# Cosformer attention and channel/token mixer on one core: the first three batches and two MLPs written as one explicit list of operations

## The chip, the cores and the metric

The kernel runs on 1 core of one Trainium2 chip. The metric is device time in microseconds (us) of one execution, the median of several. Before: 278.84 us, median of 3 runs (278.72 to 279.54). Executions of one kernel scatter by 0.7% (before, 11 runs in one set: 278.21 to 280.06) and up to 1.5% (e2: 276.80 to 280.85). A difference between two edited kernels is therefore called decided here only where their intervals do not touch.

The engines are named as in the profile: PE is TensorE, DVE is VectorE, ACT is ScalarE, POOL is GpSimd, SP is SyncE, which here only issues DMAs.

## The reference

```python
# q, k, v: 8 batches, 8 heads, 576 rows, 64 wide, f32
phi(x) = concat(relu(x) * cos_w, relu(x) * sin_w)        # 128 wide, weights by row
kv  = einsum('bhsf,bhsd->bhfd', phi(k), v)
z   = sum(phi(k), axis=2)
x   = (phi(q) @ kv) / (phi(q) . z + 1e-6)                # heads joined: 576 x 512
u   = x + (relu(x.T @ w_tok1) @ w_tok2).T                # token mixing, 576 -> 256 -> 576
out = u + relu(u @ w_ch1) @ w_ch2                        # channel MLP, 512 -> 1536 -> 512
```

## The kernel before

A batch goes through these stages: load; features of q and k (ScalarE or VectorE, 128x512 each) and a cast of v; transposes of the q features; the kv product; numerators and their division by the denominators (`x`); token mixing (`b1`, `u`); a transposed copy `uT`; then the MLP, 48 matmuls into `c_ps` (up) and 48 into `o_ps` (down). From batch 2 on, the preparation of the next batches is hooked into the slots of the running MLP. The two first MLPs had hooks of their own:

```python
    # batch 0: every stage for all heads at once
    keep_warm(34)
    for j in (3, 4, 0, 1, 2):
        s.k_feature(j, (nc.scalar, nc.scalar) if j > 2 else (None, None))
    for j in range(JA):
        s.q_feature(j, dve=(1,) if j < J else (0, 1))
    s.q_turn_mm(0)
    s.q_turn_mm(1)
    keep_warm(4)
    s.q_turn_mm(2)
    for j in range(JA):
        s.v_cast(j, nc.vector if j % 2 == 0 else nc.scalar)
    s.kv_mm(nc.vector.tensor_copy)
    # ... turns 3 and 4, num(0..4) with mix1 between them ...
    s.mix1_out(split=True)
    s.mix2_turned()          # uT of batch 0 straight from PSUM
    load_second()            # k, q, v of batch 1, then wc2, then k, q of batch 2

    def first_hooks(n, n2):                       # hooks of batch 0's MLP; n is batch 1
        # ...
        for j in range(JA):
            at(3 + j, n.k_feature, j)
            at(6 + j, n.q_feature, j, dve=(1,))
            at(10, n.v_cast, j, (nc.gpsimd, nc.gpsimd, nc.gpsimd, nc.vector, nc.scalar)[j])
        at(9, n.q_turn, 0, 2)
        at(11, n.kv_mm)
        # ...

    def second_hooks(n, m):                       # hooks of batch 1's MLP; n is batch 2, m is batch 3
        # ...
        at(5, n.kv_mm)
        at(5, load, 3, "v")
        at(5, load, 4, "k")
        at(5, load, 4, "q")
        # ...
        at(13, load, 4, "v")
        # ...
```

Loads of weights, which cast to bf16 on the way, are issued by GpSimd (by the page 3.74 MB land on its queue, for 7.47 MB of float32 weights).

## Time and profile before

| | before |
|---|---|
| time | 278.84 us |
| span of the profiled execution | 277.2 us |
| kv product of batch 0 starts | 14.70 us |
| first MLP sum (`c_ps` of batch 0) | 26.15 us |
| first output sum (`o_ps` of batch 0) | 43.37 us |
| MLP of batch 2 starts | 93.11 us |
| kv products of batches 3, 4, 5 | 93.99, 122.02, 149.60 us |

Each MLP from batch 2 on opens with its first sum and then the kv product of the next batch, so the distances between these starts are the lengths of MLP 2 and MLP 3: 28.03 and 27.58 us. Later ones also take 27.58.

From the page of the kernel before: the span, the share of TensorE, and its activity and granted clock in 40 slices of 6.9 us (9 is 90% or more).

```profile
span 277.2 us, 4630 instructions
...
PE 262.3 (95%) x1813; PEld 132.1 (48%) x1834; DVE 168.7 (61%) x333; ACT 119.7 (43%) x176; POOL 55.6 (20%) x81
...
PE   8879998998799999999999999999999999999994
...
PEclk9999999999999999999999999999999999999999
```

TensorE is nearly always busy. Apart from the last, where the kernel drains, the slices below 9 all lie in the first 76 us, so an improvement has to be found there.

From the chain of waits (start, length, what): pieces of ScalarE, and first MLP sums of TensorE (`c_ps`) as landmarks.

```profile
26.15 0.92 PE c_ps L392 x3
...
35.32 0.80 ACT qp L236
...
36.61 2.11 ACT qp L236 x3
...
43.57 1.88 ACT qpT L256
...
63.53 1.04 PE c_ps L392 x4
...
121.32 0.86 PE c_ps L392 x4
```

In these pieces TensorE waits for features and copies on ScalarE.

### The profile page before, as it was taken

The numbers are of one execution on the slowest core, as the hardware profiler recorded it, in microseconds if no ns is written. First come the engines' busy times: TensorE is split into PE (matmuls) and PEld (weight loads), VectorE is DVE, ScalarE is ACT, GpSimd is POOL, SyncE is SP. The second block draws the span as 40 slices with busy tenths as digits, with TensorE's granted clock in tenths as the row PEclk, the third lists the DMA queues.
The fourth block names the chain that finished last, engine by engine and source line by source line (L and its number), as shares of the span: only waits on it lengthen the run. The fifth ranks groups of instructions, "written<-read, shape, count | busy, mean of one in ns | idle before, by whom it ended". The sixth has DMA issues, their size and how long they took to land.

```text
span 277.2 us, 4630 instructions
## 1 busy us (share of the span) xinstructions
PE 262.3 (95%) x1813; PEld 132.1 (48%) x1834; DVE 168.7 (61%) x333; ACT 119.7 (43%) x176; POOL 55.6 (20%) x81
## 2 busy tenths in 40 slices
PE   8879998998799999999999999999999999999994
PEld 3454455444444554455445544554455444444443
DVE  4775793478549785958584859585738543423422
ACT  2882495158539247424742474248424201301300
POOL 4382340043043500610160017001100120000000
PEclk9999999999999999999999999999999999999999
DMA  6999997997999999999989968920890073003012
GB/s 206 324 171 270 362 227 198 356 346 201 185 365 316 225 214 346 231 223 279 343 155 246 311 223 116 229 95 0 148 253 20 0 116 132 0 25 129 0 63 90
DMA packets 78726, 53.62 MB, mean 193 GB/s; under 512 B 47792, under 2 KB 76016, under 8 KB 78704
## 3 DMA queue, kind: packets, MB, share of 16 engines
q1 hardware_dynamic: 74688, 49.06, 65.1%
q0 software_dynamic: 3616, 3.74, 8.5%
q10 hardware_dynamic: 400, 0.52, 0.5%
q8 instruction: 14, 0.23, 0.3%
q14 instruction: 8, 0.07, 0.1%
HBM read 35.78 MB, written 9.44 MB: 163 GB/s over the span
## 4 chain that ended last, share of the span: by engine, by line
PE 77%; ACT 9%; DMA 5%; DVE 5%; issue 2%; POOL 0%; ACTq 0%; POOLq 0%; DVEq 0%
PE c_ps L392 29%; PE o_ps L424 26%; PE b L300 5%; ACT qp L236 5%; PE u_ps L343 4%; PE nm L280 4%; DMA vt<-in_v_dram 3%; PE o_ps L404 3%; PE kv_ps L265 3%; DVE x L288 2%; DMA qpT<-qp 2%; ACT h L396 1%; ACT qpT L256 1%; PE ut_ps L355 1%; PE o_ps L416 1%
## 5 line engine op out<-in xcount | busy, mean ns | idle before, releaser
L392 PE MATMUL c_ps<-uT,wc 128*128 128x512 bf16 x384 | 93.4, 379 | 1.1 <-ACT uT L376 1.1
L396 ACT ACTIVATE h<-c_ps 128x512 bf16<-128x512 f32 x70 | 41.5, 596 | 112.7 <-PE c_ps L392 76.8
L424 PE MATMUL o_ps<-wc,h 128*128 128x512 bf16 x364 | 82.6, 379 | 0.5
L392 PEld LDWEIGHTS <-wc 128*128 128x128 bf16 x432 | 39.6, 97 | 43.9 <-issue 2.0
L424 PEld LDWEIGHTS <-h 128*128 128x128 bf16 x372 | 36.4, 98 | 43.9
L398 DVE TENSOR_SCALAR h<-c_ps 128x512 bf16<-128x512 f32 x38 | 26.1, 687 | 30.9 <-PE c_ps L392 30.9
L348 POOL CAST ub<-u 128x1024 bf16<-128x1024 f32 x14 | 14.7, 1049 | 127.1 <-DVE u L345 73.2
L427 DVE TENSOR_TENSOR u<-o_ps,u 128x512 f32<-128x512 f32 x28 | 19.2, 687 | 21.5 <-PE o_ps L424 21.5
L236 ACT ACTIVATE qp<-qt,bias,cos_t 128x512 bf16<-128x512 f32 x39 | 30.8, 803 | 0.6 <-DMA qt<-in_q_dram 0.6
L288 DVE TENSOR_TENSOR x<-nm,den 128x512 bf16<-128x512 f32 x40 | 27.7, 691 | 1.4
L223 POOL CAST vbf<-vt 128x512 bf16<-128x512 f32 x33 | 22.2, 714 | 19.4 <-DMA vt<-in_v_dram 17.9
L236 ACT ACTIVATE qp<-qt,bias,sin_t 128x512 bf16<-128x512 f32 x30 | 24.1, 802 | 0.0
L215 DVE TENSOR_SCALAR kp<-kt,cos_t 128x512 bf16<-128x512 f32 x38 | 21.3, 560 | 2.2 <-DMA kt<-in_k_dram 2.2
L345 DVE TENSOR_TENSOR u<-u_ps,x 128x1024 f32<-128x1024 f32 x16 | 19.5, 1220 | 5.1 <-PE u_ps L343 4.5
L215 DVE TENSOR_SCALAR kp<-kt,sin_t 128x512 bf16<-128x512 f32 x38 | 22.0, 580 | 0.0
L280 PEld LDWEIGHTS <-qpT 128*128 128x128 bf16 x320 | 14.6, 98 | 14.6 <-issue 4.4
L284 DVE TENSOR_SCALAR den<-nm 128x8 f32<-128x8 f32 x40 | 6.6, 165 | 24.0 <-PE nm L280 23.9
L300 PE MATMUL b<-x,w 128*128 128x512 bf16 x71 | 20.2, 379 | 0.9 <-DVE x L288 0.4
L280 PE MATMUL nm<-kv,qpT 128*128 128x65 bf16 x320 | 16.8, 194 | 3.8 <-ACT kv L270 1.4
L343 PE MATMUL u_ps<-B,w 128*128 128x512 bf16 x62 | 16.2, 379 | 0.4 <-DVE B L307 0.3
L265 PE MATMUL kv_ps<-vbf,kp 128*128 128x65 bf16 x320 | 11.8, 193 | 1.5 <-DVE vbf L223 0.8
L265 PEld LDWEIGHTS <-kp 128*128 128x128 bf16 x320 | 11.3, 97 | 3.5 <-issue 1.2
(78 smaller groups left out, 171.9 us busy)
## 6 DMA issues: line engine op xcount, KB each, us to landing
out_dram<-u SPq DMA_DIRECT2D x32, 256.0 KB, 2.6
kt<-in_k_dram SPq DMA_DIRECT2D x8, 640.0 KB, 6.2
qt<-in_q_dram SPq DMA_DIRECT2D x8, 640.0 KB, 8.6
vt<-in_v_dram SPq DMA_DIRECT2D x8, 640.0 KB, 9.5
kt<-in_k_dram SPq DMA_DIRECT2D x8, 512.0 KB, 5.3
qt<-in_q_dram SPq DMA_DIRECT2D x8, 512.0 KB, 7.3
vt<-in_v_dram SPq DMA_DIRECT2D x8, 512.0 KB, 8.8
wc<-in_moe_w_ch_dram POOLq DMA_DIRECT2D x3, 512.0 KB, 10.5
```

The costliest lines, as they stand in the source:

```text
L215: eng.tensor_scalar(dst, src, scalar1=tab, scalar2=0.0, op0=ALU.mult, op1=ALU.max)
L223: eng.tensor_copy(self.vb[:, j, :, :D], src)
L236: nc.scalar.activation(self.qp[:, j, :, f, :], src, AF.Relu, bias=bias0, scale=tab[:, self.c, j:j + 1])
L265: nc.tensor.matmul(kv_ps[:, g, hh * (D + 1):(hh + 1) * (D + 1)], self.kp[:, j, h].rearrange("p f d -> p (f d)"), self.vb[:, j, h, :D + 1], ...
L280: nc.tensor.matmul(nm[:, h // HH, c0:c0 + D + 1], lw, self.kv[:, h, :D + 1], start=True, stop=True)
L288: nc.vector.tensor_mul(self.x[:, j, :].rearrange("p (g h d) -> p g h d", g=2, h=HH), nmv[:, :, :, :D], den_b)
L300: nc.tensor.matmul(self.b1[mi], w1[self.c][:, j, mi * P:(mi + 1) * P], self.x[:, j, :], start=(j == 0), stop=(j == J))
L343: nc.tensor.matmul(u_ps[:, jj], w2[:, self.c, ki, 2 * g + jj, :], self.B1[:, ki, :], start=(ki == 0), stop=(ki == NT - 1))
L392: nc.tensor.matmul(c_ps, wc1[:, ki, mi * P:(mi + 1) * P], uT[:, :, ki, :], start=(ki == 0), stop=(ki == NCC - 1))
L396: nc.scalar.activation(h1[:, mi, :], src, AF.Relu)
L398: nc.vector.tensor_relu(h1[:, mi, :], src)
L424: nc.tensor.matmul(o_ps, h1[:, ki, j * P:(j + 1) * P], wc2[:, ki, :], start=(ki == 0), stop=(ki == NCH - 1))
```

## The change

The intent is to place each operation of the first three batches by hand. A list of words, `PLAN`, replaces the program order of the start and both special sets of hooks. A word is an operation with its arguments: `feat.0.k.3.2.0.A` is a feature of batch 0's k, row group 3, all heads, cosine half, on ScalarE (A; D is VectorE, P GpSimd); `kvm.0.0` is the kv product of four heads; `up.0.2.0.2` is the first half of the contraction of MLP row group 2; `ld.1.k.2.q12` loads batch 1's k, and its last part is a gate: not before batch 1's q has landed. Further parts: batch 0's v is loaded in head halves; q is loaded before k; token weights get one layout for both row parities (a copy by DMA and half of a GpSimd copy vanish); the first denominators get their 1e-6 from a small matmul instead of a VectorE add; MLP sums begin on half the channels.

```diff
+WARM = 20
+PLAN = """
+feat.0.q.2.2.0.D feat.0.q.0.2.1.D feat.0.q.1.2.0.A wt1.k02 feat.0.q.3.2.0.A feat.0.q.0.2.0.D feat.0.q.4.2.0.D
+feat.0.k.4.2.0.D wt2 feat.0.k.0.2.0.A feat.0.q.1.2.1.D turn.0.0.0 wu.4.4.k02 feat.0.k.4.2.1.D turn.0.0.1
+feat.0.k.2.2.1.A feat.0.k.0.2.1.D feat.0.k.1.2.1.A feat.0.q.4.2.1.D feat.0.k.3.2.0.A turn.0.2.0 turno.0.2.0.A
+turno.0.0.0.A cast.0.3.2.0.D feat.0.q.3.2.1.D feat.0.k.1.2.0.D feat.0.q.2.2.1.D turn.0.1.0 turno.0.1.0.A
+cast.0.0.3.0.P feat.0.k.3.2.1.D feat.0.k.2.2.0.D kvm.0.0 kvo.0.0.A cast.0.0.3.1.P cast.0.3.2.1.P kvm.0.1
+num.0.0.0 turno.0.0.1.D numo.0.0.0 w2a.0.A mix.0.0.0 num.0.1.0 w2a.1.P turn.0.1.1 num.0.2.0 ld.1.q.2.v01
+kvo.0.1.D num.0.0.1 turn.0.2.1 mix.0.1.0 wu.2.2.wt2 numo.0.1.0 turno.0.1.1.A mix.0.2.0 num.0.1.1 turno.0.2.1.A
+num.0.2.1 mix.0.3.0 numo.0.0.1 numo.0.2.0 mix.0.4.0 mixo.0.0.A wu.0.2.v01 wu.8.4 mix.0.0.1 feat.1.q.0.2.0.A
[... 4 lines cut ...]
+feat.1.q.3.2.1.D uto.0.2.A up.0.0.0.2 ld.1.v.0.wu2 turn.1.0.0 feat.1.q.4.2.1.D turno.1.0.0.D feat.1.q.2.2.0.A
+turno.1.0.1.D up.0.2.2.4 ld.1.v.1 turn.1.1.1 wd.9.3.k12 cast.1.4.1.0.P up.0.1.0.2 turn.1.2.0 turno.1.2.0.D
[... 22 lines cut ...]
+utx.2.0 dnj.1.0.0 feat.3.q.2.2.0.D feat.3.q.2.2.1.A turnx.3.2.2 o.1.2 dnj.1.1.1 cast.3.3.1.2.D ld.4.k.2.k22
+cast.3.1.1.2.D cast.3.4.1.2.D ld.4.v.2.k42 dnj.1.0.1 o.1.0 dnj.1.3.1 o.1.3 feat.3.k.1.2.0.A tm.2 to.2
+ld.4.q.2.v22 o.1.1
+"""
[... operations, layouts ...]
-    load(0, "k")
-    q0 = load(0, "q")
-    load(0, "v")
+    for t, g in LOADS0:                      # q, k, v of heads 0-3, v of heads 4-7
+        d = load(0, t, heads(g))
+        landed[f"{t}0{g}"] = d[1]
[... first_hooks, second_hooks and load_second removed ...]
-    for p in range(B):
+    keep_warm(WARM)
+    for word in PLAN.split():
+        name, *a = word.split(".")
+        ...
+    for p in range(2, B):
```

## The prediction

> **What bounds it now.** The page gives PE 95% busy in a 277.2 us span. The chain of waits shows two regimes. From the third batch on (c_ps at 121.3, 148.9, 176.5, 204.1, 231.7 us) each batch takes 27.58 us and the chain is nearly all PE; the change leaves that alone. Before it, the timeline has the first real matmul at 11.6 us and batch 2's MLP starting at 93.1: 81.5 us. The PE work in that stretch, by spacings in the chain (0.216 us per 512-wide matmul, 0.056 per transpose, 0.032 per 65-wide), is two MLPs 41.4, token mixing 14.7, kv and numerators 7.7, turns 6.3: 70 us. So 11 us is waiting:
> - 11.6 to 23.1, about 4.5: numerators wait for VectorE (den, reciprocal, x, 1.03 us a row group) and qpT copies; kv_ps starts at 14.7.
> - 23.1 to 63.5, about 5: ScalarE runs features and copies ahead of MLP evacuations (chain: qp L236, qpT L256, 35.3 to 45.5), then uT of batch 1.
> - 63.5 to 93.1, about 2, again ScalarE features. Another 0.6 lies in batch 2's MLP (28.2 against 27.6), which waits for qpT by DMA.
>
> **What the change does.** The same matmul work (20 tiny eps matmuls more, 0.5 us; 18 warm-up matmuls fewer, off the path). Batch 0's head, first mixing and first MLP sums go by four heads or 256 channels; features are balanced over ScalarE (0.80 us) and VectorE (0.48 us); the first denominators lose their add (0.16 us, ten row groups); w1's copy by DMA and half of w2's (4.8 us of GpSimd) vanish.
>
> **Costed on the path.**
> 1. q is loaded before k, so k should land at about 10.7, as q did. VectorE then holds 12 features and a cast before kv of heads 0-3: kv starts near 15.2, no earlier than now. Six numerator groups take 4.8 us of VectorE against 5.2. But c_ps needs only half the channels: it starts at 24 to 25 instead of 26.15, with one u_ps group (0.86) done. Gain 2 to 3.
> 2. DMA caps it: loads run at about 350 GB/s read (summary rows, casting loads counted at half). What the first four MLP row groups need (batch 0, token weights, q of batch 1, eight wc1 groups) is about 8 MB, an estimate of 25 to 27 us: short waits.
> 3. VectorE is nearly full from 15 to 40 us (about 24 us of operations), so kv of batch 1 comes near 40 to 42 and the down projection starts at 41.5 to 43 (43.4 now), with 1.2 us more done ahead.
> 4. After it, 43.5 us of PE work remains to batch 2's MLP; I expect 1.5 to 2.5 us of waits in place of 5, at u-cast-turn-copy of batch 1.
>
> Batch 2's MLP then starts at 86.5 to 89, and saves 0.5 more: 4.5 to 7 us in total. Prediction **272.5 us**, 80% range **268.5 to 277**; chances: faster by over 2% **0.56**, within 2% **0.40**, slower **0.04**.
>
> **What would show it.** kv start; first c at 24 to 25 with half the contraction; first o; start of batch 2's c_ps; later batches at 27.6 us.
>
> **What would make it wrong.** Warm-up ends near 7.3 us, and q feature j=1 stands behind a k feature on VectorE, so the first turns come near 11.5: 4 us of idle PE. [...] ScalarE's q features of batch 1 stand before the uT copies, so a late q load stalls the first MLP. If the order fits the real landing times, the gain is 8 to 9 us.

Steps 1 to 4 and the 0.5 us in batch 2's MLP come to the 4.5 to 7 us stated, and 272.5 us is 278.84 less 6.3. The rate of about 350 GB/s in point 2 is read from the page of the kernel before, whose trace shows 369 GB/s from 4 to 8 us and 359 from 8 to 12.

## More of the kernel before

All plain loads and DMA transposes, and all stores but five at the end, which ScalarE issues, are issued by SP in program order.

The next view gives stretches of the span; the first figures after the bounds are the length and TensorE's busy time, and near the end of the line stand the granted clock, the DMA share and GB/s.

```profile
14.00:18.00 4.00, 3.17 (x76) 2.80 (x73) 2.74 (x7) 4.00 (x6) 2.69 (x5) 1.00 1.04 152
...
40.00:50.00 10.00, 8.11 (x109) 5.27 (x108) 5.19 (x14) 5.55 (x7) 0.00 (x0) 1.00 0.89 218
...
70.00:80.00 10.00, 8.39 (x76) 4.13 (x74) 7.01 (x18) 3.60 (x8) 0.00 (x0) 1.00 0.97 247
```

Between 40 and 50 us TensorE is idle for 1.89 us, between 70 and 80 for 1.61. Summing all such stretches (more than are shown), TensorE idles 5.1 us from 26 to 90 us, and 3.6 from 10 to 26.

One more view, because it matters later: the SP queue while the MLPs of batches 1 to 3 run. The loads here (`kt`, `qt`, `vt`) are those of batch 4.

```profile
75.06 1.30 SPq L87 DMA_DIRECT2D kt<-in_k_dram  x2
76.41 1.90 SPq L87 DMA_DIRECT2D qt<-in_q_dram  x2
82.40 1.85 SPq L87 DMA_DIRECT2D vt<-in_v_dram  x2
...
111.25 3.54 SPq L371 DMA_TRANSPOSE uT<-ub  x2
```

Batch 4 is requested 11 to 18 us before MLP 2 starts.

The granted clock stays at 90% or more in every slice.

## The result

| | before | after | after, again |
|---|---|---|---|
| time | 279.13 us (4 runs beside it) | 277.15 us (277.07 to 278.34, 4 runs) | 277.88 us (276.46 to 279.65, 6 runs) |
| ratio to before, 95% interval | | 0.9941 (0.9918 to 0.9965) | 0.9965 (0.9934 to 0.9997) |
| span profiled | 277.2 us | 275.3 us | 275.6 us |
| kv product of batch 0 | 14.70 | 17.33 | 17.43 |
| first MLP sum | 26.15 | 28.30 | 29.69 |
| first output sum | 43.37 | 45.10 | 46.5 |
| kv of batches 3, 4, 5 | 93.99, 122.02, 149.60 | 90.45, 118.63, 148.18 | 91.83, 119.42, 148.44 |
| MLP 2, MLP 3 | 28.03, 27.58 | 28.18, 29.55 | 27.59, 29.02 |

A ratio is the mean time of one kernel's fast runs over the mean of the other's fast runs of the same rounds, so it is not quite the ratio of the medians given beside it.

The change is 0.4 to 0.6% faster. That is real, but it is about a quarter or less of the predicted 2.3%, and the first result lies just above the range. The reader should notice two things in the table: the kernel after reaches its first MLP sum *later* than before, and yet it opens MLP 2 3.5 us *earlier*; and of this 3.5 it gives 2.0 back in MLP 3, where nothing was meant to change.

The page of the kernel after, the same lines:

```profile
span 275.3 us, 4680 instructions
...
PE 260.0 (94%) x1846; PEld 133.8 (49%) x1846; DVE 169.3 (61%) x331; ACT 114.7 (42%) x181; POOL 51.1 (19%) x77
...
PE   7459999999999999997999999999999999999994
...
PEclk9959999999999999999999999999999999999999
```

The holes of slices 7, 10 and 11 are gone. Slices 2 and 3 are worse (4 and 5), the clock fell in slice 3, and a new hole stands in slice 19, near 125 us. The same stretches as before, and one more:

```profile
14.00:18.00 4.00, 1.50 (x20) 1.50 (x21) 4.00 (x5) 0.87 (x2) 2.94 (x5) 0.50 1.00 148
...
40.00:50.00 10.00, 10.00 (x120) 5.95 (x119) 7.51 (x17) 3.73 (x8) 0.00 (x0) 1.00 1.11 266
...
70.00:80.00 10.00, 10.00 (x60) 4.81 (x61) 7.64 (x16) 9.06 (x16) 1.35 (x2) 1.00 0.99 240
120.00:130.00 10.00, 8.22 (x74) 4.23 (x72) 5.62 (x16) 4.18 (x7) 0.00 (x0) 1.00 1.04 235
```

From 26 to 90 us TensorE now idles 0.08 us in all instead of 5.1. From 10 to 26 it idles 6.3 instead of 3.6, and works part of that time at half clock (0.50 from 14 to 18 us). From 120 to 130 it idles 1.78, before nothing.

**The head.** Why does the kv product start late? VectorE's timeline of the kernel after (start, length, line, operation), and below it GpSimd's in the same time:

```profile
12.67 1.17 DVE L298 TENSOR_SCALAR qp<-qt,sin_t 128x512 bf16<-128x512 f32 x1
13.77 1.72 DVE L298 TENSOR_SCALAR kp<-kt,cos_t 128x512 bf16<-128x512 f32 x1
15.40 1.04 DVE L298 TENSOR_SCALAR qp<-qt,sin_t 128x512 bf16<-128x512 f32 x1
16.37 0.83 DVE L298 TENSOR_SCALAR kp<-kt,sin_t 128x512 bf16<-128x512 f32 x1
17.12 0.47 DVE L298 TENSOR_SCALAR kp<-kt,cos_t 128x512 bf16<-128x512 f32 x1
```

```profile
14.35 2.56 POOL L259 CAST vbf<-vt 128x768 bf16<-128x768 f32 x3
```

TensorE meanwhile stands idle for 3.59 us before its next turns of q features, and starts when the third of these features is done:

```profile
16.50 1.04 PE L311 MATMUL tr<-ident,qp 128*128 128x128 bf16 x8 [3.59 <-DVE qp L298]
```

Four features that cost 0.48 us elsewhere in the same trace take 0.83 to 1.72 us each and 4.76 us together, while GpSimd runs the three v casts that the plan gave it (2.56 us). The last feature, after the casts, is back at 0.47. One feature lost more (1.72 less 0.48, or 1.24 us) than the mean of one cast (0.85). How a cast on GpSimd holds VectorE up, the trace does not show. Nor do the recorded times pair exactly: the first slow feature ends (13.84) before the casts' recorded start (14.35), while GpSimd still issues loads. That issuing alone slowed nothing in e3 below, where GpSimd issues the same loads from 11.35 to 15.03 us and four features on VectorE from 13.06 us on take 0.48 each.

**The tail.** From the chain of waits of the kernel after, around MLP 2's end:

```profile
97.68 7.51 DMA out_dram<-u
...
105.37 1.23 DVE u L438
...
112.07 5.56 DMA uT<-ub
...
117.77 1.02 PE c_ps L562 x4
...
119.74 6.03 DMA qpT<-qp
...
125.81 0.43 PE nf L357 x8
```

A store of batch 1 lands 7.5 us after its issue, VectorE's sum into that buffer waits for it, the transposes of `uT` go out late and land late, and TensorE waits 0.43 us; then it waits 1.78 us for the transposes of batch 4's q. The kernel before waited for `qpT` too, but in MLP 2 only (that is why it took 28.03); its MLP 3 had no wait. The SP queue, to compare with the lines above:

```profile
84.55 2.04 SPq L142 DMA_DIRECT2D kt<-in_k_dram  x2
91.60 1.28 SPq L142 DMA_DIRECT2D vt<-in_v_dram  x2
93.01 1.27 SPq L512 DMA_DIRECT2D out_dram<-u  x2
94.32 2.26 SPq L142 DMA_DIRECT2D qt<-in_q_dram  x2
...
98.38 2.10 SPq L142 DMA_DIRECT2D kt<-in_k_dram  x2
...
107.79 6.99 SPq L445 DMA_TRANSPOSE uT<-ub  x2
```

Batch 4's loads went out 9 to 18 us later than before, two of them after MLP 2's start at 89.6 us, so they and batch 5's loads (from 98.38) are in flight together, with the stores between them. The cause in the list, tested in e5, is this: `ld.4.v` waits until k of batch 4 has landed, and `ld.4.q` stands behind that wait in the same queue.

### The profile page after: what moved, and what is told of

It is laid out like the page before. It is cut to its first block, busy times and chain, and to the rows that moved or that the text cites. A ratio compares the mean times of both kernels' runs of the same rounds, so it can differ in the third digit from the quotient of the medians.

```text
span 275.3 us, 4680 instructions
## 1 busy us (share of the span) xinstructions
PE 260.0 (94%) x1846; PEld 133.8 (49%) x1846; DVE 169.3 (61%) x331; ACT 114.7 (42%) x181; POOL 51.1 (19%) x77
## 4 chain that ended last, share of the span: by engine, by line
PE 65%; DMA 7%; DVE 3%; SPq 1%; issue 0%; POOL 0%; DVEq 0%
PE c_ps L562 22%; PE o_ps L579 22%; PE b L406 4%; PE c L485 4%; PE o L497 4%; PE u L433 3%; DMA out_dram<-u 3%; PE kv L327 2%; PE nf L357 2%; DMA qpT<-qp 2%; DMA uT<-ub 2%; PE o_ps L571 1%; DVE u L438 1%; PE ut L461 1%; DVE x L383 1%; SPq L445 0%
## 5 line engine op out<-in xcount | busy, mean ns | idle before, releaser
L562 PE MATMUL c_ps<-uT,wc 128*128 128x512 bf16 x288 | 70.4, 379 | 0.4 <-DMA uT<-ub 0.4
L259 POOL CAST ub<-u 128x1024 bf16<-128x1024 f32 x14 | 15.2, 1086 | 124.9 <-issue 62.7
L259 POOL CAST vbf<-vt 128x512 bf16<-128x512 f32 (+3 forms) x28 | 19.8, 743 | 24.3 <-DMA vt<-in_v_dram 24.3
L296 ACT ACTIVATE qp<-qt,cos_t 128x512 bf16<-128x512 f32 x31 | 21.9, 712 | 5.0 <-DMA qt<-in_q_dram 5.0
L485 PE MATMUL c<-uT,wc 128*128 128x512 bf16 x96 | 23.1, 379 | 0.0
L497 PE MATMUL o<-wc,h 128*128 128x512 bf16 x96 | 22.3, 379 | 0.0
L296 ACT ACTIVATE qp<-qt,sin_t 128x512 bf16<-128x512 f32 x31 | 21.5, 710 | 0.7 <-DMA qt<-in_q_dram 0.7
L406 PE MATMUL b<-x,w 128*128 128x512 bf16 (+1 forms) x90 | 20.5, 355 | 1.0 <-DVE x L383 1.0
L383 DVE TENSOR_TENSOR x<-nf,den 128x512 bf16<-128x512 f32 x30 | 20.7, 692 | 1.0
L438 DVE TENSOR_TENSOR u<-u,x 128x1024 f32<-128x1024 f32 x16 | 19.4, 1219 | 2.3 <-PE u L433 1.6
L433 PE MATMUL u<-B,w 128*128 128x512 bf16 x64 | 16.3, 379 | 0.0
```

The costliest lines, as they stand in the source:

```text
L259: (nc.scalar.copy if eng == "A" else ENG[eng].tensor_copy)(dst, src)
L296: nc.scalar.activation(dst, src, AF.Relu, scale=tab)
L383: nc.vector.tensor_mul(dst, nmv[:, :, :, :D], den_b)
L406: nc.tensor.matmul(b1[:, mi], w1[:, col(self.c, j), mi * P:(mi + 1) * P], self.x[:, j, cs], start=(j == 0 and (g == 2 or mi == 0)), stop=( ...
L433: nc.tensor.matmul(ps[:, jj], w2[:, ki, 1 + 2 * g + jj, :], self.B1[:, ki, :], start=(ki == 0), stop=(ki == NT - 1))
L485: nc.tensor.matmul(ps, wc1[:, ki, mi * P:(mi + 1) * P], self.uT[:, :, ki, :], start=(ki == 0), stop=(ki == NCC - 1))
```

## The experiments

First theory (from the traces): three things eat the gain. (a) GpSimd casts hold up VectorE in the head; (b) the idle gaps of the head (2.53 and 3.59 us) lower the clock (0.50 from 14 to 18 us); (c) batch 4's loads, gated at the end of the list, collide with the next ones. Rival: DMA bytes, or TensorE's own work, are the floor of the first 45 us, so that a better head gains nothing. All kernels below are edits of the kernel after. "MLP 2 + 3" is the distance from the kv product of batch 3 to that of batch 5; 55.17 is twice 27.58.

| run | time, us | ratio (95%) | kv, batch 0 | first c | first o | kv, batch 3 | MLP 2 + 3 |
|---|---|---|---|---|---|---|---|
| before | 278.84 | 1 | 14.70 | 26.15 | 43.37 | 93.99 | 55.61 |
| after | 277.15 | 0.9941 (0.9918–0.9965) | 17.33 | 28.30 | 45.10 | 90.45 | 57.73 |
| c_after_again | 277.88 | 0.9965 (0.9934–0.9997) | 17.43 | 29.69 | 46.5 | 91.83 | 56.61 |
| e1_early_loads | 278.13 | 0.9957 (0.9936–0.9977) | 17.95 | 29.55 | 46.44 | 94.47 | 55.18 |
| e2_keep_clock | 278.20 | 0.9972 (0.9936–1.0007) | 17.69 | 30.51 | 48.97 | 94.31 | 57.61 |
| e3_casts_scalar | 276.97 | 0.9923 (0.9898–0.9947) | 15.22 | 28.02 | 45.84 | 91.18 | 58.15 |
| e4_whole_sums | 277.63 | 0.9952 (0.9919–0.9984) | 18.21 | 30.94 | 47.06 | 92.40 | 56.50 |
| e5_ungated_tail | 276.83 | 0.9924 (0.9905–0.9944) | 18.23 | 30.98 | 47.78 | 93.12 | 55.17 |
| e6_tail_and_casts | 276.22 | 0.9908 (0.9886–0.9930) | 15.56 | 28.02 | 46.41 | 93.19 | 55.17 |
| e6_again | 276.78 | 0.9923 (0.9909–0.9937) | 15.63 | 28.68 | 46.51 | 91.85 | 55.17 |
| e7_whole_v1 | 279.32 | 1.0006 (0.9964–1.0048) | 17.90 | 29.47 | 47.62 | 93.01 | 58.40 |
| e8_head_mended | 276.91 | 0.9937 (0.9904–0.9970) | 15.57 | 27.87 | 46.06 | 92.40 | 55.17 |
| e9_fewer_bytes | 275.45 | 0.9868 (0.9850–0.9887) | 15.54 | 27.62 | 45.87 | 91.63 | 55.16 |
| e9_again | 275.45 | 0.9878 (0.9852–0.9903) | 15.37 | 27.89 | 46.21 | 91.56 | 55.16 |
| e10_ungated_k1 | 276.84 | 0.9913 (0.9882–0.9944) | 15.32 | 29.10 | 46.99 | 92.33 | 55.17 |
| e11_head_and_k1 | 276.66 | 0.9908 (0.9877–0.9939) | 14.96 | 28.05 | 46.38 | 91.72 | 55.17 |
| e11_again | 276.77 | 0.9925 (0.9911–0.9940) | 15.30 | 28.86 | 47.09 | 92.43 | 55.17 |
| e12_weights_in_order | 276.45 | 0.9918 (0.9873–0.9963) | 15.42 | 27.03 | 46.47 | 91.81 | 55.17 |
| e13_fewer_and_k1 | 276.38 | 0.9917 (0.9897–0.9938) | 15.88 | 29.29 | 47.41 | 92.76 | 55.17 |

Times are medians of 4 runs (after; before is its first 3), 5 (e9_fewer_bytes) or 6 (all others). e1 to e4 ran in one set of rounds, c_after_again and e5 to e7 in a second on the same chip, e8, e9 and e6_again in a third, e10 to e12 in a fourth, e9_again, e11_again and e13 in a fifth; the ratios are to the kernel before in the same rounds. "The control" is c_after_again. It ran beside e5 to e7 only, so all others are compared with it by their ratios. Milestones are those of the one profiled execution. They scatter: five kernels whose head up to there has the same code (after, c_after_again, e1, e5, e7) gave 28.30 to 30.98 for the first MLP sum, so a single milestone there is read to about 2.7 us. Landings scatter too: k of batch 0 came at 10.35 us in after and at 11.26 in e5, with the same code up to there. The last column is stiff, to a tenth, where TensorE does not wait in MLP 2 and 3. e9 and e13 compute a wrong result; all others were correct.

### The unedited kernel again

> The changed kernel itself, unedited, beside the edits of this job on the same chip. The earlier runs of one kernel scattered from 277.07 to 278.34, and in the traces of the first job k of batch 0 landed anywhere from 10.35 to 11.2 us with the same code. If that scatter is ordinary: 277.1 to 278.3, ratio 0.994.

Measured: 277.88 us, MLP 2 + 3 in 56.61 us, with 1.26 us of waiting for the transposes of q in MLP 3. The loss in the tail is not an accident of one trace, but it varies (2.2 us of waits in the first trace).

### e1: batch 4's k and q much earlier

```diff
-ld.3.v.2.wd3 ...
+ld.3.v.2.wd3 ld.4.k.2 ld.4.q.2 ...
-... ld.4.k.2.k22 / ld.4.v.2.k42 / ld.4.q.2.v22
+... ld.4.v.2
```

> The changed kernel with only the six loads of batch 4 moved: k and q are issued right after v of batch 3 (about 73 us) instead of at the very end of the list (84.5 to 96.6), v without its gate. Theory A (the list ends with its own stretch, so it leaves batch 4's loads to the end, and they queue in front of the uT and qpT transposes of batch 3, which costs the third batch 0.6 and the fourth 2.1 us): batches 2 and 3 take about 27.6 and 27.7 us instead of 28.0 and 29.7, and the kernel takes 274.5 us instead of 277.1 (ratio to before 0.984). Rival (the transposes are slow because the DMA engines are full in this stretch whatever the order): the waits only move, total within 0.5 us of 277.1.

Measured: MLP 2 + 3 falls to 55.18, so the tail's loss is gone, but the time, 278.13 us, is no better than the control. In the SP queue the two transposes of `qpT` that follow these loads now take 10.13 us, and the `uT` transposes of batch 2 behind them move from 80.25 to 88.75:

```profile
78.53 10.13 SPq L320 DMA_TRANSPOSE qpT<-qp  x2
88.75 2.67 SPq L445 DMA_TRANSPOSE uT<-ub  x2
```

The same two transposes took 5.77 us in the kernel after. TensorE waits 1.54 us ahead of MLP 2's first sum (by the profile for VectorE's `u`). The expected 274.5 us was missed. So (c) is right about the place, and this mend is wrong: the loads were put ahead of more urgent transposes. That this is where the gain went is read from one trace.

### e2: keep the clock up

```diff
-WARM = 20
+WARM = 32
-... turn.0.1.0 ...
+... wm.14 turn.0.1.0 ...        # 14 empty matmuls ahead of the last turns
```

> The changed kernel with 12 more warm-up matmuls at the start and 14 in front of the fourth turn, where TensorE stood idle (8.9 to 11.4 and 12.9 to 16.5 us). If the half clock between 13 and 19 us costs time on the path: clock mean 1.0 instead of 0.988, 40 kv matmuls in 1.45 instead of 2.38 us, first MLP sum 0.7 to 1.0 us earlier than 28.3, kernel 276.2 us. If VectorE's numerators set the pace of the head: clock 1.0 and the kernel within 0.3 us of 277.1.

Measured: the clock of the profiled execution rises to 0.994 (0.988 after), that of the other five is 1.00, and the 40 kv matmuls no longer run at half rate (1.6 us instead of 2.38). The time is 278.20 us, not better than the control. In the profiled execution ScalarE waited for q of batch 1, which landed at 28.65 us, and the first MLP sum came at 30.51, after TensorE had waited 2.19 us for `uT`; but this execution was the slowest of the six (280.85 us, the others 276.80 to 278.35), so its milestones are not typical. The clock's fall is real, and undoing it alone buys nothing that these six runs can show.

### e3: the v casts on ScalarE

```diff
-cast.0.0.3.0.P cast.0.0.3.1.P cast.0.3.2.1.P
+cast.0.0.3.0.A cast.0.0.3.1.A cast.0.3.2.1.A      # placed by the early turno's
```

> The changed kernel with only the three casts of batch 0's v moved from GpSimd to ScalarE, which stands idle for 3.1 us there. If the GpSimd casts are what stretches the VectorE features beside them from 0.48 to 0.8-1.7 us: those features go back to 0.48, kv starts at about 15.8 instead of 17.3, the first MLP sum comes 1 to 1.5 us earlier, kernel 275.8 us. If q of batch 1 (needed on ScalarE ahead of the uT copies, landed at 25.8) or the weights hold the first MLP: kv starts early all the same, but the gain at the first MLP sum and at the end is under 0.5 us.

Measured: VectorE's features in the same stretch:

```profile
13.06 0.48 DVE L298 TENSOR_SCALAR qp<-qt,sin_t 128x512 bf16<-128x512 f32 x1
13.46 0.48 DVE L298 TENSOR_SCALAR kp<-kt,cos_t 128x512 bf16<-128x512 f32 x1
13.85 0.48 DVE L298 TENSOR_SCALAR qp<-qt,sin_t 128x512 bf16<-128x512 f32 x1
14.25 0.48 DVE L298 TENSOR_SCALAR kp<-kt,sin_t 128x512 bf16<-128x512 f32 x1
```

All are back at 0.48, and the kv product starts at 15.22, where I had predicted it. So (a) is shown: it was the casts on GpSimd. But the first MLP sum still comes at 28.02, and the time, 276.97 us, lies within the control's scatter. Of the two microseconds gained at 15 us, at most a part is left there: e3, e6 and e6_again, with the casts moved, have the first sum at 28.02 to 28.68, the five with the old head at 28.30 to 30.98. By the first output sum (45.84 to 46.51 against 45.10 to 47.78) the two groups cannot be told apart. TensorE works at a clock of 0.50 here from 12.8 to about 23 us, which may hold part of it.

### e4: MLP sums over all channels at once

```diff
-up.0.2.0.2 up.0.3.0.2 ... up.0.0.0.2 ... up.0.1.0.2       # first halves
-up.0.2.2.4 ... up.0.0.2.4 ... up.0.1.2.4 ... up.0.3.2.4
+up.0.2     ... up.0.0     ... up.0.1     ... up.0.3
```

> The changed kernel with one part undone: the first four MLP sums of batch 0 wait for all 512 channels instead of beginning on half of them. If beginning on half is worth what I put on it, TensorE loses up to 8 matmuls' time (1.7 us) around 28 to 31 us: kernel 278 to 278.8. If TensorE finds other work in the meantime, under 0.5 us: 277.1 to 277.6.

Measured: first MLP sum at 30.94, which says nothing, since e5 has 30.98 with the half sums. The time is 277.63 us, ratio 0.9952, against 0.9965 of the control. The half-channel sums, a named part of the change, are worth nothing that can be measured in the total.

### e5: batch 4's loads without gates, in place

```diff
-ld.4.k.2.k22 ... ld.4.v.2.k42 ... ld.4.q.2.v22
+ld.4.k.2 ld.4.q.2 ... ld.4.v.2
```

> Batch 4's three loads stay behind all transposes of the list, where they are, but lose the waits on one another, and q goes directly after k: k, q, v at 84.5 to 90 us instead of 84.5 to 96.6. The first job's early loads removed the loss in batches 2 and 3 (27.6 and 27.6 us) but pushed the uT transposes of batch 2 from 80.3 to 88.8 us. Theory A (it is the queue's order that costs the 2.7 us): batches 2 and 3 near 27.7 and 28.2 us without the stall at batch 2's first MLP sum, kernel 275 us, ratio 0.987. Rival (the DMA engines are full, so only the place of the wait changes): no better than the unedited kernel of this job, within 0.5 us.

Measured: 276.83 us against 277.88 for the control in the same rounds, MLP 2 + 3 in 55.17 us and no wait of TensorE in MLP 2 or 3. The SP queue:

```profile
86.62 2.00 SPq L142 DMA_DIRECT2D kt<-in_k_dram  x2
88.67 1.31 SPq L142 DMA_DIRECT2D qt<-in_q_dram  x2
90.07 1.97 SPq L142 DMA_DIRECT2D vt<-in_v_dram  x2
...
109.95 3.58 SPq L445 DMA_TRANSPOSE uT<-ub  x2
```

In this execution MLP 2 started at about 92.3, so all three loads are out before it; in the kernel after, v and q followed 2 and 5 us behind its start. The transposes take 3.58 us in the queue as in the kernel before, not 6.99. Every later kernel with this edit shows the same 55.17 to within a hundredth. The six traces with the gated tail (after, c_after_again, e2, e3, e4, e7) show TensorE waits of 1.2 to 2.7 us in MLP 2 and 3, and none with this edit shows any. That is the evidence for the tail's cause; it does not separate the gates from the place of q, which the edit also moves ahead of v. The gain in the total is only just seen: the intervals (0.9905 to 0.9944, control 0.9934 to 0.9997) overlap by a thousandth. In the kernel after, SP waited 5.0 us for the landing of k ahead of the load of v (91.60 us), and the load of q stood behind that wait in the same queue (94.32).

### e6 and e6_again: e5 and e3 together

> Ungated tail and the v casts on ScalarE together. If a faster head is swallowed because k and v of batch 1 land at 34 to 36 us and kv of batch 1 can start only at 42 whatever the head does: same as the ungated tail alone within 0.5 us. If the head's 2 us come through once the tail is mended: 1.5 us less than the ungated tail alone.

> The ungated tail with casts again, as the best so far and as the control of this job: 276.2 us, ratio 0.991.

Measured: 276.22 and 276.78 us, ratios 0.9908 and 0.9923. The first interval does not touch that of the control of the same rounds (0.9934 to 0.9997). This is a correct version that beats the kernel before by about 0.8% and the control by 0.4 to 0.6%; the interval of the repeat (0.9909 to 0.9937), from other rounds, overlaps the control's by a hair.

### e7: batch 1's v whole instead of in halves

```diff
-ld.1.v.0.wu2 ... ld.1.v.1 ... (gates v10, v11)
+ld.1.v.2.wu2 ...              (gates v12)
```

> One named part undone: v of batch 1 is loaded whole instead of in two head halves. kv of batch 1 starts at 42 us, after the k features (k lands at 33.7), and v's second half has landed by 38: I expect no difference, within 0.5 us of the unedited kernel. If the half load is what lets kv start: kv of batch 1 1 to 2 us later and the kernel 1 us slower.

Measured: 279.32 us, level with the kernel before and slower in the median than the control, but their intervals overlap (0.9964 to 1.0048, control 0.9934 to 0.9997), so this is not decided. The whole v lands at 38.9 us, everything gated on it goes out later, and the profiled execution waits in MLP 2 and 3 for `uT` (0.81) and twice for `qpT` (0.73 and 1.16). The profiled execution was a slow one (280.41 us, of 277.62 to 281.39). I had expected no difference. That the halves matter, and do so through the gates behind them, is my reading of this one trace and is not shown.

### e8: the head mended

e5 and e3, with warm-up matmuls (32 at the start, 9 ahead of the last turns) and with two features of batch 1 moved behind the first `uT` copies, so that ScalarE does not wait for q of batch 1 ahead of them.

```diff
-wu.8.4 mix.0.0.1 feat.1.q.0.2.0.A / ux.0.0 feat.1.q.0.2.1.A / um.0.0 ... uto.0.1.D
+wu.8.4 mix.0.0.1 / ux.0.0 / um.0.0 uto.0.1.D feat.1.q.0.2.0.A feat.1.q.0.2.1.A ...
```

> Ungated tail and v casts on ScalarE, and now also the clock kept (12 more warm-up matmuls, 9 in front of the fourth turn) and both uT copies ahead of batch 1's q features on their engines. First MLP sum at about 25.5 us instead of 28.0. If the loads set a floor (k of batch 1 lands at 34 to 36 us, its features follow, kv near 42): kv of batch 1 stays at 41.5 to 42.5, the stretch from first MLP sum to first down projection grows from 18 to 20 us, and the kernel is no faster than the same without these two edits (within 0.5 us of the repeat in this job). If the head is what limits: 2 us faster than the repeat.

Measured: 276.91 us against 276.78 for e6_again in the same rounds. First MLP sum 27.87, first output sum 46.06. Both kernels start the kv product at 15.6, so this comparison tests the clock and ScalarE's order only, and these gain nothing that can be measured. My first theory explains the start at 17.33 but not the total.

One thing was overlooked here. From the first MLP sum to MLP 2 TensorE takes 61.28 to 61.29 us almost without waiting in after (0.08 us of idle), c_after_again and e5, but 62.29 in e3, 62.31 in e6_again, 63.67 in e8 and 64.31 in e6. Part of what the mended head gains is lost there. One of these waits, in the second half of batch 1's kv product, shows in e3, e6, e6_again and e8 (0.61, 0.71, 0.63 and 0.42 us; the last figures here are e8's):

```profile
43.33 0.81 PE L332 MATMUL kv<-vbf,kp 128*128 128x65 bf16 x20 [0.42 <-DVE u L443]
```

The wait is for VectorE's sum `u`. In e3, e6_again and e8 VectorE's cast of batch 1's v takes 1.51 us instead of 0.68 while GpSimd casts v beside it, so the collision of the head seems to return there; but e6 has its cast in 0.67 us and waits as long. e6 and e8 also wait for the down weights, 1.28 and 0.84 us near 52 us. What delays `u` stays open; no experiment tests it.

### e9: 1 MB less to load

```diff
-wu.8.4                                        # last third of the first MLP weights
+nc.gpsimd.memset(wc1[:, :, 8 * P:], 0.0)      # wrong result on purpose
```

> Wrong result on purpose: the mended head, with the last third of the first channel weight (1 MB of reads) not loaded but set to zero, so that k and v of batch 1 follow 1 MB sooner. If the loads are the floor: k lands about 2.5 to 3 us earlier (31 to 33 us), kv of batch 1 and the first down projection come 1.5 to 3 us earlier than with all bytes, kernel 1.5 to 2.5 us faster than the mended head. If something else (features on VectorE, TensorE itself) holds kv near 42: under 0.5 us.

> The same kernel as e9_fewer_bytes, for the same chip and rounds: 275 to 276 us, ratio 0.985 to 0.989, k of batch one landing at about 34 us because its load still waits for q's landing. Both theories expect the same.

Measured: 275.45 us twice, ratios 0.9868 and 0.9878, against 0.9937 of e8 and 0.9923 of e6 beside it. So leaving this load out saves time, about 1.3 us. (The edit also removes one load issue from GpSimd and adds a memset there; this is not separated from the bytes.) But the milestones moved less than that: the first MLP sum is at 27.62 and 27.89, and there TensorE waits 0.69 and 1.12 us *for the weights that are left*:

```profile
27.89 1.04 PE L491 MATMUL c<-uT,wc 128*128 128x512 bf16 x4 [1.12 <-DMA wc<-in_moe_w_ch_dram]
```

So in some executions a head that gets there early finds the weights missing (`wu.2.2`, gated on the token weights; here they land at 27.6 us or later). It is not the reason in all: e3, e6, e6_again and e8, with all bytes, show no wait for these weights. Around that landing the DMA engines are half idle, because k of batch 1 waits for the landing of q (window, as above; DMA share 0.48 and 80 GB/s at the end of the line, 1.07 and 376 in the next 4 us):

```profile
26.00:30.00 4.00, 2.68 (x18) 1.19 (x16) 2.49 (x4) 2.61 (x6) 0.00 (x0) 1.00 0.48 80
```

### e10, e11, e12: k of batch 1 without its gate, and weights in order of use

e10 is e6 with `ld.1.k.2` in place of `ld.1.k.2.q12`; e11 is e8 with it; e12 is e11 with the first MLP's weight pieces loaded in the order in which they are used.

```diff
-wu.4.4.k02 ... wu.2.2.wt2 ... wu.0.2.v01
+wu.2.2.k02 wu.0.2 ... wu.4.4.wt2             # e12 only
```

> Ungated tail and casts (276.2 to 276.8 before) with one more wait removed: k of batch 1 is issued right after q of batch 1 instead of when that has landed. If this wait is what holds the middle: k lands at 29 to 31 us instead of 34.5, kv of batch 1 starts near 39 to 40 instead of 42.4, the first down projection 1 to 2 us earlier than 46.5, kernel 275 us. If the DMA engines are simply full: k lands at 32 to 34, the weights of the first MLP later by as much, kernel within 0.5 us of 276.5.

> The mended head (276.9) with the same wait removed. If head and middle were each hiding the other: first MLP sum 26 to 28, first down projection near 44, kernel 274.5 us. If the loads bound both: within 0.5 us of the ungated k alone.

> As the one before, with the first channel weight's pieces loaded in the order in which they are used (256 columns twice, then 512 twice). If the first MLP sum waits for its weights (27.3 to 27.6 us in the traces with a faster head): first MLP sum 0.5 to 1 us earlier and up to 0.5 us at the end. If q of batch 1 and TensorE set it: no difference within 0.5 us.

Measured: 276.84, 276.66 and 276.45 us: all the same within the noise, and the same as e6. k of batch 1 lands earlier in e10 (32.9 us instead of 33.7 or more), but not in e11 (34.5) and e12 (34.3). TensorE now waits for weights 1.6 us (e10) and 2.6 us (e11). In e12 the first sum comes at 27.03 without a wait, the earliest of all, and the wait turns up at another piece, 1.26 us at 36.1. In these single traces, reordering loads moved the wait from one delivery to another.

### e13 and e11_again: fewer bytes and no gate

> e11 (tail, head and k of batch one ungated) without the load of the last third of the first MLP weights, which are set to zero instead: a wrong result on purpose. If the bytes of the opening stretch are the floor, k of batch one lands at about 31 us instead of 33 to 36, the projections of batch one start at 39.5 to 40.5 us, the first output sums at about 44 us, and the time is 273.5 to 274.5 us, at least 1 us below e9. If loads are not the floor and TensorE's own work before batch two is, the first output sums stay at 45.5 to 46.5 us and the time stays at e9's 275 to 275.7 us.

> The same kernel as e11_head_and_k1 for the same rounds: 276.3 to 277 us, TensorE waiting 1.5 to 2.6 us for the last third of the first MLP weights. The difference to e13 is what these 1 MB of the opening stretch cost.

Measured: e13 276.38 us, e11_again 276.77 us (with 3.4 us of waits for weights, more than I expected), beside e9_again 275.45 us. Both expectations for e13 missed: it is neither at 274 nor at e9's time. k lands at 33.1 us, not at 31, and TensorE waits for weights twice:

```profile
29.29 1.04 PE L491 MATMUL c<-uT,wc 128*128 128x512 bf16 x4 [0.94 <-DMA wc<-in_moe_w_ch_dram]
...
32.57 0.61 PE L491 MATMUL c<-uT,wc 128*128 128x512 bf16 x2 [1.14 <-DMA wc<-in_moe_w_ch_dram]
```

With k let loose, the weights come 1.4 us later than in e9_again (29.29 against 27.89); 0.5 of that stands already at the landing of batch 0's k (11.14 against 10.62), before the edit acts. The intervals of the two kernels (0.9897 to 0.9938 and 0.9852 to 0.9903) overlap slightly. My reading is that neither bytes alone nor TensorE's work alone are the floor, but the landing of the pieces that TensorE's fixed order asks for next, and that the gate on k, which looked like a mistake in e9, protects the weights of the first MLP. It rests on these two traces and is not shown by the times.

## Why the prediction was wrong

I predicted 272.5 us, with a range up to 277. It came out at 277.15 and, again, 277.88.

**What was right.** The place: the change acts before MLP 2, and the MLPs from the fifth on are untouched. The kv product of batch 1 started at 41.98 (predicted 40 to 42), but this is partly luck: the head was late, and the repeat has 43.37. The down projection, in the same step, came at 45.10 instead of 41.5 to 43: from first MLP sum to first output sum took 16.80 us without a wait (predicted 17 to 18), so the lateness of step 1 was carried through. The cure of the middle: I had counted on 1.5 to 2.5 us of waits between the first output sum and MLP 2 in place of 5; there were 0.08 from 26 us on. From the first output sum to MLP 2 it took 44.5 us, predicted 45 to 46; here the waits were fewer and the work (44.4 us) more than the 43.5 predicted. The listed dangers of the head came true: TensorE idles 2.5 and 3.6 us around its first turns. The clock falls as well, to 0.50 in the stretch from 14 to 18 us. It fell at 12.7 us, after 2.53 us of idle (8.85 to 11.38) and 1.3 us into the transposes that followed, before the gap of 3.59 us began. With both gaps filled (e2) it stayed at 1.00 in five of six runs; how long a gap it takes, no run here shows. ScalarE waited for q of batch 1 (it landed at 25.8 us) ahead of the `uT` copies.

**Step 1 failed: "kv starts near 15.2 ... it starts at 24 to 25 instead of 26.15 ... Gain 2 to 3".** The kv product started at 17.33 and the first MLP sum at 28.30, a loss of 2.2. I costed VectorE's features at 0.48 us and the casts on GpSimd as free. They stretched four features by 2.8 us in sum (4.76 less four times 0.48); e3 gave 15.22 back by moving the casts. From the kv product to the first sum the step then took 10.97 us, where 9 to 10 were predicted: TensorE idled 1.05 of it and ran at a clock of 0.50 to 19.5 us. And a good head is not the whole of the step: in e9, e9_again and e11 TensorE had to wait for the weights of the first sum, until 27.6 to 28.1 us.

**Step 2 was too mild for a mended head: "25 to 27 us: short waits".** In the kernel after itself TensorE waited for no weights at all, since the head was late. I added up bytes and divided by a rate (350 GB/s; the kernel after moved 372 from 30 to 34 us); in the runs with a mended head the order of landing counted too. The weights of the first sum are the second piece in the list and gated on another landing, and in the runs where TensorE waited for them they came at 27.6 to 29.3 us.

**The tail was left out.** I expected half a microsecond saved in MLP 2 and MLP 3 unchanged at 27.58 ("the change leaves that alone"). MLP 2 took 28.18, and MLP 3 29.55. e5 shows the cause: how the list issues batch 4's loads (the gates, and v ahead of q). The rule that I broke is that a list which replaces hooks also replaces the *loads for later batches* that those hooks issued.

**The sum.** Predicted gain 278.84 less 272.5, or 6.3 us; measured 2.0 (279.13 less 277.15). In the profiled executions, MLP 2 started at 89.59 and not at my 87.75: 1.8 us. MLP 2 took 0.15 longer than before instead of 0.5 less: 0.65. MLP 3 took 1.97 longer. After MLP 3, 0.5 was won that I had not predicted (spans 1.9 us apart, kv of batch 5 only 1.42). That makes 4.0 of the missing 4.3; the rest is that my stages add up to 5.9 us and not to 6.3. (87.75 is the middle of the predicted 86.5 to 89.)

**Where the head's potential went.** With the tail and the casts both mended (e6, e6_again) the kernel takes 276.22 and 276.78 us, still about 4 us above the predicted 272.5. So the two causes that are shown explain the milestones and the waits, not the whole of the miss in time. A head whose kv product starts 2 us earlier gains at most 0.4% (e3 against the control), or 0.2% in the same rounds (e6 against e5), both with overlapping intervals. TensorE runs one fixed order with at least three outside deliveries in it: weights of the first sum (27.0 to 29.3 us), k of batch 1 (33 to 36), v of batch 1 (35 to 39). In e10, e11_again and e13 k landed earlier (32.8 to 33.1 us) and TensorE waited for weights; in e12 the first weights were hastened and another piece came late. Each of these is one trace, and in the mended heads that waited for no first weights (e3, e6, e6_again, e8) the longer stretch after the first sum, told under e8, takes part of the gain. So the cause is in part open. Open too is where e9 saves its 1.3 us: its two profiled executions (276.06 and 275.98 us) were slower than its medians of 275.45, that of e6_again (276.24) faster than its median of 276.78, so the profiles differ by less than the medians. Nor did I find an order of loads that turns the head's 2 us into time.

The best correct versions are e6, e8 and e10 to e12 (276.2 to 276.9 us), 0.6 to 0.9% faster than before. Among them nothing is decided.

## What to carry to other kernels

When hooks are replaced by an explicit order, follow every load that the old hooks issued for *later* stages to its new place, and compare its issue time with the moment when the queue must be free for urgent transposes (the two of `uT` held it 6.99 us here instead of 3.54). Where several deliveries fed one in-order engine, moving one of them earlier moved the wait here (1.6 us for the weights in e10, 1.26 us at another piece in e12); cost a faster stage against the landing of its next input, not against its own work. An operation given to an idle engine is not free if it slows another engine, as the casts on GpSimd did (features of 0.48 us took 0.83 to 1.72): look at how long the neighbour's instructions take while it runs.
